# Passing the last two token groups through layer 1 together, 512 tokens wide, with 20 blocks of layer 2 converted beside it

## The chip, the core and the metric

The kernel runs on one core of one Trainium2 chip. The metric is device time in microseconds (us): the median of several executions. The core has five engines with a queue each: TensorE (PE, whose weight loads are shown as PEld), VectorE (DVE), ScalarE (ACT), GpSimd (POOL) and the sync engine (SP), which here only issues DMAs. Each queue runs in order. DMAs move data between DRAM and the on-chip memory; matmuls write to PSUM, of which there are eight banks of 512 fp32 columns.

## What is computed

Attention with a hash mask, and behind it two feed-forward layers, all in float32:

```python
# q, k, v: (2, 8, 768, 64); proj: (64, 6)
q_bucket, k_bucket = bits(q @ proj > 0), bits(k @ proj > 0)
scores = where(q_bucket == k_bucket, q @ k.T / 8, -1e9)
x = (softmax(scores) @ v).reshape(1536, 512)           # 1536 tokens
# layer 1: w_gate, w_val (512, 1536), w_out (1536, 512)
g = x @ w_gate
x = (g * sigmoid(g) * (x @ w_val)) @ w_out
# layer 2: w_in (512, 2048), w_out (2048, 512)
h = x @ w_in
out = (max(h, 0) + alpha * min(h, 0)) @ w_out
```

## The kernel before

**Attention.** There are 24 items: batch b, token group g of 256 tokens (three of them per batch) and pair p of heads, the pair running fastest. An item has two units, one per head, 48 in all. A unit goes through `banks` (three score banks in PSUM, each copied by ACT into the unit's tile `se`, in L280), `top` (maximum over keys on DVE, transposed on TensorE), `back` (subtract on DVE, exponential on ACT) and `values` (three pieces of the product with V, into the tile `po`). That makes eight steps per unit, and the parts of neighbouring units are interleaved. `prep` gives a pair its keys and hash rows. A pair's K comes three times: as one tile `nat` (SP's queue, L161) and twice into `kt` (POOL's queue); `rest_k` (L173) subtracts one from the other. For the pairs 1 to 3 of batch 0 `nat` is taken from the ring `se` of four buffers, in which the units' scores lie as well; for batch 1 it has a buffer of its own.

**Layer 1.** Six groups g of 256 tokens. Weights come as blocks of 128 x 512, 36 of them for layer 1 (24 for gate and value, 12 for output) and 32 for layer 2. Every product is made of three fp32r matmuls (`mm3`: high x high, high x low, low x high), so that a block has a high and a low half (tile `wb`, 512 KB, five buffers). In group 0 the blocks are converted from 64-bit storage: loaded as `raw` (ring `raw64` of two buffers), put together by `round64` (ACT L501, DVE L502 and L504, POOL L506), split (ACT L530; POOL or DVE L537) and stored to `scratch` in DRAM; the later groups load `wb` from there on SP's queue (L496). A step f of `stage1` uses two gate and value blocks and, from f = 3 on, one output block: 12 matmuls each, 432 in a group.

**What runs beside what.** Groups 0 to 4 are interleaved with attention: `stage1` yields 36 times in a group, and at each yield as many steps of attention are emitted as `RATES` says (2.0). A group begins when its tokens' attention is done. Besides, 18 blocks of layer 2 are converted early, six in each of the groups 2 to 4 (`EARLY`, `w_early`): `raw` load, `round64` into a tile `wt`, write to `whole` in DRAM (L525). Group 5 runs alone.

**Layer 2.** `stage2` passes three times over 512 tokens. Its 32 blocks are kept in `fin.w` (tile `w`): 18 are loaded from `whole` (L492), and the other 14 are loaded raw and converted in the first pass. In each pass a block is split again into `wb`.

**Order.** The Tile scheduler puts each engine's instructions into an order, by its own estimate. Instructions under `pin` keep the program's order; `ws.pin` is False while attention and layer 1 are interleaved, except for the early blocks. `w_ahead` issues weight loads three blocks ahead of use for blocks already in scratch.

## Time and profile before

| | us |
|---|---|
| median of 3 runs | 944.65 (941.87 to 944.72) |
| the profiled execution, its own time | 942.76 |
| its span, first to last instruction | 940.8 |
| TensorE busy (matmul) | 859.9 |
| VectorE busy | 593.6 |
| ACT busy | 442.6 |
| POOL busy | 389.3 |

A busy TensorE is not TensorE at its peak, since the matmuls are pipelined and their ends modelled: what a matmul costs is the distance from one start to the next. The stages in the profiled execution, by the first and the last matmuls of each: attention alone until 90.5 us, group 0 of layer 1 until 248.7, group 1 until 341.8, group 2 until 437.9, group 3 until 531.9, group 4 until 615.5, group 5 until 670.2, and the three passes of layer 2 until 762.7, 849.8 and 937. Attention's last matmul is in group 4. The table by stages below gives for each stretch its length, how long each engine was busy in it and with how many instructions, TensorE's granted clock and what the DMAs moved.

### The profile page before, as it was taken

The numbers are of one execution on the slowest core, as the hardware profiler recorded it, in microseconds if no ns is written. First come the engines' busy times: TensorE is split into PE (matmuls) and PEld (weight loads), VectorE is DVE, ScalarE is ACT, GpSimd is POOL, SyncE is SP. The second block draws the span as 40 slices with busy tenths as digits, with TensorE's granted clock in tenths as the row PEclk, the third lists the DMA queues.
The fourth block names the chain that finished last, engine by engine and source line by source line (L and its number), as shares of the span: only waits on it lengthen the run. The fifth ranks groups of instructions, "written<-read, shape, count | busy, mean of one in ns | idle before, by whom it ended". The sixth has DMA issues, their size and how long they took to land.

```text
span 940.8 us, 14038 instructions
## 1 busy us (share of the span) xinstructions
PE 859.9 (91%) x5248; PEld 765.6 (81%) x5248; DVE 593.6 (63%) x880; ACT 442.6 (47%) x784; POOL 389.3 (41%) x339
## 2 busy tenths in 40 slices
PE   4788787787999999999999997799999999999998
PEld 3577675676898999999999997789887788888886
DVE  4589999998665767677767752131489754335342
ACT  4588565745544554555555441121344433334331
POOL 4224666556433213233223312211478845444442
PEclk8799989989999999999999999899999999999999
DMA  9324767778999767878787867799934010001001
GB/s 236 73 68 134 227 232 218 251 232 268 321 305 298 228 214 242 279 262 280 246 269 235 269 224 290 278 358 362 366 114 155 1 46 1 0 1 45 1 1 45
DMA packets 70403, 180.53 MB, mean 192 GB/s; under 512 B 18880, under 2 KB 25024, under 8 KB 70336
## 3 DMA queue, kind: packets, MB, share of 16 engines
q1 hardware_dynamic: 68176, 174.10, 55.4%
q0 software_dynamic: 2016, 5.51, 2.9%
q8 instruction: 41, 0.67, 0.3%
q14 instruction: 26, 0.21, 0.1%
q10 hardware_dynamic: 144, 0.05, 0.0%
HBM read 152.88 MB, written 26.74 MB: 191 GB/s over the span
## 4 chain that ended last, share of the span: by engine, by line
PE 62%; DVE 16%; DMA 9%; POOL 5%; issue 4%; ACT 4%; SPq 1%; POOLq 0%; DVEq 0%; ACTq 0%
PE po L317 9%; PE gp L592 5%; PE gp L594 5%; PE gp L593 5%; PE hp L594 4%; PE op L599 4%; PE op L597 4%; PE op L598 4%; PE hp L592 4%; PE hp L593 4%; DMA nat<-in_k_dram 3%; DMA raw<-in_wblk_dram 3%; PE yp L594 3%; PE yp L592 2%; PE yp L593 2%
## 5 line engine op out<-in xcount | busy, mean ns | idle before, releaser
L587 POOL TENSOR_TENSOR gl<-ex,gh 128x256 fp32r<-128x256 f32 (+1 forms) x120 | 121.6, 1013 | 265.2 <-ACT gh L584 198.5
L592 PE MATMUL gp<-xh,wb 128*128 128x256 f32 x576 | 177.5, 308 | 18.4 <-ACT wb L530 11.4
L594 PE MATMUL gp<-xh,wb 128*128 128x256 f32 x576 | 168.3, 292 | 6.8 <-POOL wb L537 4.8
L593 PE MATMUL gp<-xl,wb 128*128 128x256 f32 x576 | 166.5, 289 | 1.8 <-POOL xl L346 1.8
L317 PE MATMUL po<-se,vv 128*128 128x256 f32 x576 | 149.8, 396 | 6.5 <-issue 3.5
L592 PEld LDWEIGHTS gp<-xh,wb 128*128 128x128 f32 x576 | 113.1, 196 | 24.7 <-ACT wb L530 14.5
L317 PEld LDWEIGHTS po<-se,vv 128*128 128x128 f32 x576 | 106.6, 199 | 19.8 <-ACT se L310 4.8
L594 PEld LDWEIGHTS gp<-xh,wb 128*128 128x128 f32 x576 | 113.3, 197 | 10.8 <-POOL wb L537 7.0
L593 PEld LDWEIGHTS gp<-xl,wb 128*128 128x128 f32 x576 | 113.5, 197 | 3.0 <-POOL xl L346 2.0
L584 ACT ACTIVATE gh<-ex 128x256 fp32r<-128x256 f32 (+1 forms) x120 | 60.2, 502 | 118.1 <-DVE ex L581 62.5
L310 ACT ACTIVATE se<-se 128x1536 f32<-128x1536 f32 x48 | 71.3, 1484 | 63.5 <-DVE se L305 63.3
L530 ACT ACTIVATE wb<-w 128x512 fp32r<-128x512 f32 x96 | 59.5, 628 | 83.4 <-PE hp L594 55.2
L592 PE MATMUL yp<-gh,wb 128*128 128x256 f32 x288 | 87.3, 305 | 11.6 <-DMA wb<-w 8.1
L537 POOL TENSOR_TENSOR wb<-w,wb 128x512 fp32r<-128x512 f32 x48 | 65.9, 1374 | 74.3 <-ACT wb L530 72.2
L506 POOL TENSOR_TENSOR wt<-wt,wr 128x512 int32<-128x512 int32 x54 | 76.5, 1416 | 48.5 <-DVE wt L504 31.1
L280 ACT ACTIVATE se<-S 128x512 f32<-128x512 f32 x144 | 80.1, 592 | 20.7 <-PE S L279 12.6
L572 DVE SCALAR_TENSOR_TENSOR ex<-ex,gp 128x256 f32<-128x256 f32 x72 | 30.1, 418 | 93.2 <-ACT ex L569 92.7
L537 DVE TENSOR_TENSOR wb<-w,wb 128x512 fp32r<-128x512 f32 x48 | 45.1, 940 | 66.5 <-ACT wb L530 66.5
L305 DVE SCALAR_TENSOR_TENSOR se<-se,mb 128x1536 f32<-128x1536 f32 x48 | 83.8, 1745 | 4.4 <-PE mb L300 4.2
L594 PE MATMUL yp<-gh,wb 128*128 128x256 f32 x288 | 82.2, 291 | 2.7 <-POOL wb L537 1.6
L593 PE MATMUL yp<-gl,wb 128*128 128x256 f32 x288 | 82.0, 286 | 0.5 <-POOL gl L587 0.5
L278 PE MATMUL S<-QA,kt 128*128 128x256 f32 x288 | 78.8, 301 | 1.9 <-ACT se L280 0.9
(92 smaller groups left out, 1943.5 us busy)
## 6 DMA issues: line engine op xcount, KB each, us to landing
wb<-w SPq DMA_DIRECT2D x180, 512.0 KB, 4.9
raw<-in_wblk_dram SPq DMA_DIRECT2D x68, 512.0 KB, 4.4
w<-wb SPq DMA_DIRECT2D x36, 512.0 KB, 5.2
qr<-in_q_dram SPq DMA_DIRECT2D x24, 256.0 KB, 4.4
kt<-in_k_dram POOLq DMA_DIRECT2D x14, 384.0 KB, 8.5
whole<-wt SPq DMA_DIRECT2D x18, 256.0 KB, 2.2
w<-whole SPq DMA_DIRECT2D x18, 256.0 KB, 5.4
nat<-in_k_dram SPq DMA_DIRECT2D x8, 384.0 KB, 7.9
```

Of the source, the lines that this page charges most:

```text
L278: nc.tensor.matmul(pt[:, i, :], lhsT=ka[:, sl], rhs=qa, start=True, stop=False)
L280: nc.scalar.activation(out=u.se[:, 2 * j:2 * j + 2, :], in_=pt, func=AF.Copy)
L305: nc.vector.scalar_tensor_tensor(out=u.se, in0=u.se, scalar=FLOOR, in1=u.mx[:, None, :].to_broadcast([P, NC, GQ]), op0=ALU.max, op1=ALU.su ...
L310: nc.scalar.activation(out=u.se, in_=u.se, func=AF.Exp, scale=SCALE)
L317: nc.tensor.matmul(it.po[:, u.x, :], lhsT=VV[it.b, it.p][:, kb, u.x * D:u.x * D + P], rhs=u.se[:, kb, :], start=kb == 0, stop=kb == NC - 1)
L506: pin(nc.gpsimd.tensor_tensor(out=a, in0=a, in1=r, op=ALU.add))
L537: eng.tensor_tensor(out=ready[i][:, 1, :], in0=wt.pop(i), in1=f32(ready[i])[:, 0, :], op=ALU.subtract)
L584: nc.scalar.activation(out=h, in_=ex, func=AF.Copy)
L587: nc.gpsimd.tensor_tensor(out=l, in0=ex, in1=f32(h), op=ALU.subtract)
L592: nc.tensor.matmul(pt, lhsT=h, rhs=ah, start=first, stop=False)
L593: nc.tensor.matmul(pt, lhsT=h, rhs=al_, start=False, stop=False)
L594: nc.tensor.matmul(pt, lhsT=l, rhs=ah, start=False, stop=last)
```

## The change

- `nat` of the pairs 1 to 3 of batch 0 is a buffer of the ring `raw64` (two buffers in the pool `wp`), no longer of `se`.
- `RATES` has four entries, 2.0, 2.4, 2.6 and 2.6; `EARLY` is 0, 0, 6, 6: four groups are interleaved with attention, and 12 blocks are converted early, in the groups 2 and 3.
- The groups 4 and 5 go through layer 1 together, in the new `stage1w`, after attention. Each matmul is 512 columns wide, 432 in all, with the weights loaded once for both groups.
- The other 20 blocks of layer 2 (`late`) are converted beside it by `w_late`, two per step f for ten steps, straight into `fin.w`, with two blocks' loads in the air; `w_load` does nothing for them. Loads and conversions there are pinned. The first pass of layer 2 converts nothing.

```diff
@@ -38,9 +38,9 @@
 
 PRIME = (32, 6)
 
-RATES = (2.0, 2.0, 2.0, 2.0, 2.0)
-
-EARLY = (0, 0, 6, 6, 6, 0)
+RATES = (2.0, 2.4, 2.6, 2.6)
+
+EARLY = (0, 0, 6, 6)
 
 
 @with_exitstack
@@ -156,8 +156,10 @@
 
     def load_k(it):
 
-        tag, n = ("se", at.nse) if it.b == 0 else ("nat", 1)
-        it.nat = at.sm.tile([P, S], F32, tag=tag, name="nat", bufs=n)
+        if it.b == 0:
+            it.nat = wp.tile([P, S], F32, tag="raw64", name="nat", bufs=RAWB)
+        else:
+            it.nat = at.sm.tile([P, S], F32, tag="nat", name="nat", bufs=1)
         nc.sync.dma_start(out=it.nat, in_=kview2(it))
         nc.gpsimd.dma_start(out=KA(it)[0:D], in_=kview(it))
         nc.gpsimd.dma_start(out=KB(it)[0:D], in_=kview(it))
@@ -463,7 +465,8 @@
 
     o2 = order2()
     early = o2[:sum(EARLY)]
-    seq = order1() * (B * NG) + o2 * NP2
+    late = [w for w in o2 if w not in early]
+    seq = order1() * (len(RATES) + 1) + o2 * NP2
     NWT = len(seq)
     fresh = [w not in seq[:i] for i, w in enumerate(seq)]
     new = [n or w >= F2I for n, w in zip(fresh, seq)]
@@ -488,8 +491,10 @@
 
     def w_load(i):
         w = seq[i]
-        if fresh[i] and w in early:
-            nc.sync.dma_start(out=fin.w[:, w - F2I, :], in_=whole[w - F2I])
+        if w in late:
+            pass
+        elif fresh[i] and w in early:
+            pin(nc.sync.dma_start(out=fin.w[:, w - F2I, :], in_=whole[w - F2I]))
         elif fresh[i]:
             raw[i] = raw_load(w)
         elif w < F2I:
@@ -513,6 +518,17 @@
             wt[i] = wp.tile([P, 512], F32, tag="wt", name="wt", bufs=WB[0])
         if i in raw:
             round64(raw.pop(i), wt[i].bitcast(I32))
+
+    def w_late():
+
+        rs = []
+        for w in late + [None] * RAWB:
+            if len(rs) == RAWB or w is None:
+                r, v = rs.pop(0)
+                round64(r, fin.w[:, v - F2I, :].bitcast(I32))
+            if w is not None:
+                rs.append((raw_load(w), w))
+            yield
 
     def w_early():
 
@@ -659,6 +675,43 @@
             nc.scalar.activation(out=xh[:, 2 * i:2 * i + 2, :], in_=yp[i], func=AF.Copy)
             nc.vector.tensor_tensor(out=xl[:, 2 * i:2 * i + 2, :], in0=yp[i], in1=f32(xh)[:, 2 * i:2 * i + 2, :],
                                     op=ALU.subtract)
+
+    def stage1w(t0):
+
+        xh, xl = [t[:, :, t0:t0 + W] for t in X]
+        gs = {}
+        conv = w_late()
+        for f in range(F1 + D1):
+            for _ in range(-(-(len(late) + RAWB) // F1)):
+                next(conv, 0)
+            if f < F1:
+                ps = []
+                for i in range(2):
+                    tag = ("G", "M", "G", "po")[(2 * f + i) % 4]
+                    pt = at.ps.tile([P, W], F32, tag=tag, name="gp2", bufs=at.nb[tag])
+                    w = w_next()
+                    for kk in range(KD):
+                        mm3(pt, (w[0][:, kk, :], w[1][:, kk, :]), xh[:, kk, :], xl[:, kk, :], kk == 0, kk == KD - 1)
+                    ps.append(pt)
+                ex = tmp()
+                gs[f] = [fin.pool.tile([P, W], F32R, tag=t, name=t, bufs=D2 + 1) for t in ("gh2", "gl2")]
+                gate_tanh(ps[0], ex)
+                gate_mul(ps[0], ex)
+                gate_val(ps[1], ex)
+                split_h(gs[f][0], ex)
+                split_l(gs[f][0], gs[f][1], ex)
+            if f >= D1:
+                fo = f - D1
+                h, l = flat(w_next())
+                a, b_ = gs.pop(fo)
+                if fo == 0:
+                    yp = [at.ps.tile([P, W], F32, tag=t, name="yp2", bufs=at.nb[t]) for t in "SSYY"]
+                for e in range(KD):
+                    sl = slice(e * P, (e + 1) * P)
+                    mm3(yp[e], (h[:, sl], l[:, sl]), a, b_, fo == 0, fo == F1 - 1)
+        for e in range(KD):
+            nc.scalar.activation(out=xh[:, e, :], in_=yp[e], func=AF.Copy)
+            nc.vector.tensor_tensor(out=xl[:, e, :], in0=yp[e], in1=f32(xh)[:, e, :], op=ALU.subtract)
 
     def stage2(t0):
 
@@ -764,8 +817,8 @@
         pass
     fin.pool = ctx.enter_context(tc.tile_pool(name="fin", bufs=1))
     fin.w = fin.pool.tile([P, 2 * F2, 512], F32, name="w2")
-    for _ in stage1(B * NG - 1):
-        pass
+    ws.pin = True
+    stage1w(len(RATES) * GQ)
     for n in range(NP2):
         stage2(n * W)
```

What the scheduler makes of it, at two places.

The start, on SP: the loads behind the first two items. nat_154, nat_200 and nat_208 are the K tiles of the pairs 1 to 3, nat_2248 that of batch 1, vv the tiles of V, qr those of Q, al alpha. Before:

```order
L155 DMA vv_160<-in_v_dram 128x6x64 x2
L161 DMA nat_200<-in_k_dram 128x768
L161 DMA nat_208<-in_k_dram 128x768
L167 DMA qr_216<-in_q_dram 128x2x256
L122 DMA al_69<-in_alpha_dram 128x16
L161 DMA nat_2248<-in_k_dram 128x768
L155 DMA vv_204<-in_v_dram 128x6x64 x2
L155 DMA vv_212<-in_v_dram 128x6x64 x2
L155 DMA vv_218<-in_v_dram 128x6x64 x2
L167 DMA qr_299<-in_q_dram 128x2x256
```

After:

```order
L155 DMA vv_160<-in_v_dram 128x6x64 x2
L163 DMA nat_200<-in_k_dram 128x768
L122 DMA al_69<-in_alpha_dram 128x16
L169 DMA qr_216<-in_q_dram 128x2x256
L163 DMA nat_2248<-in_k_dram 128x768
L155 DMA vv_204<-in_v_dram 128x6x64 x2
L155 DMA vv_212<-in_v_dram 128x6x64 x2
L155 DMA vv_218<-in_v_dram 128x6x64 x2
L163 DMA nat_208<-in_k_dram 128x768
L169 DMA qr_299<-in_q_dram 128x2x256
```

nat_208 moved from the place behind nat_200 to one behind the six loads of V.

The start, on ACT: the score copies of the first unit (se_222) and of the second (se_256), and the exponentials (L310 before, L312 after). Before:

```order
L280 ACTIVATE se_222<-S_230 128x512
L280 ACTIVATE se_222<-S_237 128x512
L178 ACTIVATE QA_340<-qr_216 128x512
L310 ACTIVATE se_222<-se_222 128x1536
L280 ACTIVATE se_256<-S_257 128x512
L280 ACTIVATE se_256<-S_263 128x512
L280 ACTIVATE se_256<-S_274 128x512
L201 ACTIVATE kt1_128<-mk_280 12x384 x2
```

After:

```order
L282 ACTIVATE se_222<-S_230 128x512
L282 ACTIVATE se_222<-S_237 128x512
L282 ACTIVATE se_256<-S_257 128x512
L282 ACTIVATE se_256<-S_263 128x512
L282 ACTIVATE se_256<-S_274 128x512
L180 ACTIVATE QA_340<-qr_216 128x512
L312 ACTIVATE se_222<-se_222 128x1536
L312 ACTIVATE se_256<-se_256 128x1536
```

The second unit's copies moved ahead of the first unit's exponential.

The end of the last group that runs beside attention and the start of what follows it, on SP. w18 to w35 and then w0, w1, ... are layer 1's blocks in scratch, raw64 the raw loads, whole the write of an early block. Before, from group 4 to group 5:

```order
L525 DMA whole_109<-wt_6415 128x512
L496 DMA wb_6458<-w33_106 128x1024
L496 DMA wb_6473<-w34_107 128x1024
L486 DMA raw64_6495<-in_wblk_dram 128x1024
L496 DMA wb_6497<-w35_108 128x1024
L496 DMA wb_6511<-w0_73 128x1024
L496 DMA wb_6531<-w1_74 128x1024
L496 DMA wb_6545<-w2_75 128x1024
L525 DMA whole_109<-wt_6525 128x512
L496 DMA wb_6568<-w3_76 128x1024
L496 DMA wb_6583<-w4_77 128x1024
```

After, from group 3 to the wide stage:

```order
L501 DMA wb_5873<-w2_75 128x1024
L541 DMA whole_109<-wt_5853 128x512
L489 DMA raw64_5896<-in_wblk_dram 128x1024
L489 DMA raw64_5898<-in_wblk_dram 128x1024
L501 DMA wb_5901<-w3_76 128x1024
L501 DMA wb_5916<-w4_77 128x1024
L489 DMA raw64_5943<-in_wblk_dram 128x1024
L489 DMA raw64_5950<-in_wblk_dram 128x1024
L501 DMA wb_5953<-w5_78 128x1024
L501 DMA wb_5968<-w6_79 128x1024
L489 DMA raw64_5995<-in_wblk_dram 128x1024
L489 DMA raw64_6002<-in_wblk_dram 128x1024
```

Where weight loads alone stood after the last early block, two raw loads now stand ahead of each step's weight loads, and the last writes to whole come in group 3.

## Rows read from the trace of the kernel before

**Rows 1.** Busy by stretch: length, PE, PEld, DVE, ACT, POOL (instructions), clock, DMA share, GB/s.

```profile
20.00:43.00 23.00, 15.53 (x56) 10.23 (x55) 11.81 (x15) 8.94 (x14) 6.16 (x3) 0.67 0.51 130
43.00:90.50 47.50, 41.46 (x245) 35.17 (x244) 43.44 (x69) 39.89 (x70) 13.62 (x12) 0.96 0.27 87
90.50:248.70 158.20, 126.45 (x753) 108.49 (x753) 145.96 (x202) 95.09 (x169) 98.41 (x81) 0.91 0.77 243
...
341.80:437.90 96.10, 94.92 (x706) 91.33 (x705) 71.46 (x113) 53.97 (x101) 30.90 (x28) 1.00 0.75 255
437.90:531.90 94.00, 93.97 (x702) 90.92 (x701) 67.55 (x108) 51.02 (x91) 27.77 (x25) 1.00 0.76 255
561.00:615.50 54.50, 42.68 (x312) 41.61 (x311) 12.97 (x29) 11.37 (x26) 13.52 (x15) 0.91 0.75 281
615.50:670.20 54.70, 52.63 (x434) 51.98 (x433) 11.50 (x26) 10.93 (x28) 8.90 (x13) 1.00 0.97 356
622.00:662.00 40.00, 39.95 (x333) 39.78 (x332) 8.43 (x20) 7.59 (x19) 6.30 (x9) 1.00 0.98 359
670.20:762.70 92.50, 88.64 (x386) 71.76 (x386) 72.65 (x81) 40.06 (x69) 68.62 (x48) 1.00 0.34 118
762.70:849.80 87.10, 87.10 (x386) 72.13 (x385) 36.24 (x50) 31.52 (x51) 41.16 (x32) 1.00 0.04 13
```

**Rows 2.** DMA issues, 622 to 662 us: count, size, median us to landing.

```profile
wb<-w SPq DMA_DIRECT2D x27, 512.0 KB, 5.2
```

**Rows 3.** The chain that ended last, in order of time: start, us, what.

```profile
556.01 5.23 PE po L317 x24
```

**Rows 4.** Timeline of SP's queue, 545 to 690 us: start, us, what is issued.

```profile
566.36 0.32 SPq L525 DMA_DIRECT2D whole<-wt  x1
...
567.26 2.60 SPq L496 DMA_DIRECT2D wb<-w  x4
...
615.59 0.32 SPq L525 DMA_DIRECT2D whole<-wt  x1
```

**Rows 5.** Instructions by line, PE, 561 to 616: busy, mean ns, idle before.

```profile
L592 PE MATMUL gp<-xh,wb 128*128 128x256 f32 x61 | 19.1, 313 | 4.5 <-DMA wb<-w 4.5
...
L592 PE MATMUL yp<-gh,wb 128*128 128x256 f32 x44 | 13.2, 299 | 7.3 <-DMA wb<-w 7.3
```

**Rows 6.** Timeline of PE, 570 to 576 us, after a wait for a weight block.

```profile
573.92 0.35 PE L592 MATMUL yp<-gh,wb 128*128 128x256 f32 x1 [2.98 <-DMA wb<-w]
...
575.06 0.42 PE L593 MATMUL yp<-gl,wb 128*128 128x256 f32 x1
575.27 0.41 PE L594 MATMUL yp<-gh,wb 128*128 128x256 f32 x1
```

**Rows 7.** Timeline of the start, 15 to 40 us: start, us, engine, line, what.

```profile
15.62 11.03 SPq L155 DMA_DIRECT2D vv<-in_v_dram  x6
...
18.19 1.24 ACT L280 ACTIVATE se<-S 128x512 f32<-128x512 f32 x2 [0.43 <-PE S L279]
...
26.25 5.46 PE L317 MATMUL po<-se,vv 128*128 128x256 f32 x12 [3.47 <-issue]
...
31.81 1.58 ACT L280 ACTIVATE se<-S 128x512 f32<-128x512 f32 x3 [5.66 <-PE po L317]
...
32.92 0.69 DVE L284 TENSOR_TENSOR m<-se 128x512 f32<-128x512 f32 x1 [5.42 <-ACT se L280]
...
37.63 1.74 DVE L305 SCALAR_TENSOR_TENSOR se<-se,mb 128x1536 f32<-128x1536 f32 x1
```

**Rows 8.** Instructions by line, 670 to 763 us: layer 2's first pass, with conversions.

```profile
L506 POOL TENSOR_TENSOR w<-w,wr 128x512 int32<-128x512 int32 x14 | 20.2, 1440 | 10.0 <-DVE w L504 5.7 <-ACT wr L501 2.3 <-ACT wb L530 2.0
L504 DVE SCALAR_TENSOR_TENSOR w<-raw,w 128x512 int32<-128x512 int32 x14 | 17.4, 1244 | 0.3
L502 DVE TENSOR_SCALAR w<-raw 128x512 int32<-128x512 int32 x14 | 11.4, 813 | 2.6 <-DMA raw<-in_wblk_dram 2.5
L581 DVE SCALAR_TENSOR_TENSOR ex<-hp,ex 128x512 f32<-128x512 f32 x16 | 11.0, 688 | 0.4
```

## The prediction

> **What bounds the kernel now.** I read the span by stages first [rows 1], then who ends the waits in the stages that lose time [rows 3 to 6], then the start [rows 7]. The reader is to see that TensorE is the bound from 248.7 us on, except in three stretches.
>
> Two prices come first. From 622 to 662 us one group passes layer 1 alone: 333 matmuls of 256 columns in 40.00 us, 0.120 us each. The second pass of layer 2 needs 87.10 us for 384 matmuls of 512 columns (16 blocks x 4 x 3, twice), 0.2268 us each [rows 1].
>
> Group 3 of layer 1, with attention beside it (437.9 to 531.9 us), is TensorE and nothing else: busy 93.97 of 94.00 us [rows 1]. Its own 432 matmuls are 51.8 us, and 42.2 us belong to 72 steps of attention. VectorE is busy 67.55 us there. Group 0 (90.5 to 248.7) is bound by VectorE, 145.96 of 158.2 us, and so is the tail of the start: 43.44 of 47.5 us from 43 to 90.5 [rows 1].
>
> Attention ends at 561.2 us (the last run of matmuls into po, [rows 3]). From there to 615.5 us only 312 matmuls run, 37.4 us of work in 54.5; from 615.5 to 670.2 us 434, 52.1 us in 54.7 [rows 1]. The 17.1 us lost in the first stretch have one shape. A converted block is written to DRAM (whole<-wt) by SP's queue, five of them there, from 566.36 to 615.59 us; the queue stands at that write until GpSimd has finished the block, and the weight loads (wb<-w) stand behind it [rows 4]. TensorE then waits for wb, 7.3 + 4.5 us in all [rows 5], and after such a wait of 2.98 us its matmuls start 0.21 us apart (575.06, 575.27) [rows 6], the lower of the clock's two levels; the granted clock is 0.91 over the stretch [rows 1]. So one such block costs 17.1 / 5 = 3.4 us. The first pass of layer 2 takes 92.50 us, 5.4 over the second [rows 1]: TensorE waits there for weights whose split stands behind conversions on VectorE and GpSimd.
>
> **The change part by part.** All sums stand against the profiled execution, 942.76 us (span 940.8 and 2.0 around it). The median of the runs is 944.65, 1.9 above it, and one of the three is 0.9 below, so the sum may sit some 2 us low.
>
> *K of three pairs in the raw64 ring.* Before, the three early K tiles and the first unit's scores fill the four buffers of se, so the second unit's scores are copied only at 31.81 us, when ACT has idled 5.66 us for the first unit's po, and VectorE idled 5.42 us for that [rows 7]. In the new order these copies follow directly on the first unit's, which end at 19.4 us: 12 us sooner. Still in its place is the first unit's po, from 26.25 to 31.7 us on TensorE [rows 7] at a granted clock of 0.67 over 20 to 43 us [rows 1], and the next pair's hash behind it. What goes is VectorE's work on the second unit, five instructions from 32.92 to 39.37 us [rows 7], 0.69 + 0.69 + 0.42 + 0.42 + 1.74 = 4.0 us, that now falls into idle time, and about 1 us of waits in its chain. From 20 to 43 us VectorE worked 11.81 of 23 us, after that 91% [rows 1], so whatever its start gains lasts. Between 0 and the idle 11.2 us I take 5, which is nearest to the 4.0 just counted. The cost: the load of the last early K (nat_208) now waits for a buffer and stands behind six loads of V whose issue takes 11.03 us, from 15.62 to 26.65 us [rows 7]. Issued at 26.7 and with some 5 us to land [rows 2] it is there at about 32 us, an estimate; the instructions behind it on VectorE are the next pair's hash, which need that pair's matmuls, not before 31.8 us. If it lands later, the 5 us shrink.
>
> *Attention 2.4 to 2.6 steps per step of layer 1.* In the program's order 1851 of the 2592 matmuls of layer 1 stand before the last one of attention; in the changed order 1575 of the 256-wide kind. TensorE is the bound, so attention ends 276 x 0.120 = 33.1 us earlier, and nothing is saved by that itself. VectorE gets denser: even if all of group 2's 71.46 us [rows 1] scaled by 1.3, it would be 92.9 us beside 51.8 + 1.3 x 42.2 = 106.7 us of TensorE, 87%. That is under the 92% of group 0, where TensorE did idle. I charge 1 us, bounded by 0 and by 3.5 (group 2's 96.10 - 94.92 = 1.2 us idle [rows 1], in each of some 96 of 280 us).
>
> *What is left after attention.* Before: 741 matmuls, 88.9 us of work, in 109.2 us: 20.3 us lost. After: 153 matmuls of 256 columns (18.4 us) and 432 of 512 columns (98.0 us), 116.4 us of work, where the same was 33.1 + 88.9 = 122.0: 5.7 us saved by the width (864 x 0.120 = 103.7 against 98.0). The trace shows a fixed part of 2 x 0.120 - 0.2268 = 0.013 us per matmul that wider ones pay half as often [rows 1].
>
> The Trainium skill, "TensorE: Matmul & The Clock Gate", section Back-to-back issue gap, gives N/2.4 + 2.5 ns for a matmul at full clock. By that an estimate of the saving is 432 x 2.5 ns = 1.1 us, and the sum would come 4.6 us higher, at 921. The trace does not agree with its fixed part (13 ns against 2.5), and the measured one is used.
>
> Lost time after: three whole<-wt writes still stand behind attention's end in SP's order, but the last has only 512-wide blocks ahead of it (12 x 0.2268 = 2.7 us each, three loaded), which cover it. Two at 3.4 us are 6.8 us; bounds 3.4 and 10.3 (one and three).
>
> *Twenty blocks converted beside the wide stage.* One step of it is 36 matmuls, 8.2 us; the first three lack the output block, 5.4 us. Per step two blocks: VectorE 2 x 0.69 us for the gates (the nearest form of that width) and 2 x (0.81 + 1.24) for the conversions, 5.5 us; GpSimd three additions of 1.44, 4.3 us [rows 8]. Both lie under 8.2 us of TensorE and are just even with it in the first three steps. SP: each raw load waits until VectorE and ACT have read the block two before it, which comes behind the last step's gate, and the next step's weight load stands behind both. From the end of a value matmul: gate 0.7, conversions to +2.8 and +4.8, weights landing 5.2 us later [rows 2], +10; needed at +10.9, four blocks of 2.7 us later (in the first three steps three blocks, +8.2). So a wait of a us or so in some of the first steps, none later. DMA: five blocks of 524288 bytes per step, 2.62 MB in 8.2 us = 321 GB/s, under the 359 moved from 622 to 662 us [rows 1]. I charge 2 us. The lower bound is 0; the upper is the 281 GB/s of 561 to 615.5 us [rows 1], 9.3 us per step, +1.2 in each of ten steps: 12 us. If the cover of 8.2 us were gone, the ten pairs would cost VectorE's 10 x 4.1 = 41 us.
>
> *First pass of layer 2.* Its 14 conversions are gone, and so 5.4 us of waits [rows 1]; loads from whole fall from 18 to 12. I take 5.0 (0.4 left for a late first load), bounds 3 and 5.4.
>
> Sum: 942.8 - 5 (start) + 1 (denser attention) - 5.7 (width) - (20.3 - 6.8 - 2 = 11.5) (waits after attention) - 5.0 (first pass) = 916.6, say **917 us**.
>
> **The rivals.** *Late blocks stall like early ones* (slower than before). If SP's queue stands at each raw load as it stands at whole<-wt, twenty blocks cost 3.4 us each: 914.6 + 68 = 983 us. It decides from (942.8 - 914.6) / 20 = 1.4 us a block. For it: the loads do wait on VectorE. Against: there is no write that waits for GpSimd; a raw load waits for reads that end some 5 us after the gate, where the writes stood (615.59 - 566.36) / 4 = 12.3 us apart [rows 4], the time of a block from its load to its end. 5 in 100.
>
> *DMA is the bound of the wide stage*, at the 281 GB/s above: 916.6 - 2 + 12, about 927 us. For it: bursts of five loads per step, writes are gone though. 17 in 100.
>
> *The change at the start does not do what it says*: the late K holds VectorE's queue as long as the second unit gained, or longer by up to 3 us: 922 to 925. 10 in 100.
>
> *More than forecast*: the start gives 9 us and only one early block stalls (3.4): 909. 13 in 100.
>
> **How the numbers follow.** My forecast, 917, has 55 in 100. The range 905 to 932 us takes in the rivals at 909, 925 and 927 with some 5 us for bounds that fall together; it leaves out the first rival and sums where several terms go to their ends. About 0.3% (2.8 us) can be told from no change here. Of the first rival's 5, 4 are slower by more and 1 falls within; one more within comes from the DMA case with all else at its bad end. So faster 0.94, same 0.02, slower 0.04.
>
> **What would show it.** Right: second unit's score copies near 19.5 us and group 0 starting near 85; attention ending near 523; group 3's tail losing 5 to 8 us; the wide stage 98 to 101 us long with the clock at 1.0 and DMA near 320 GB/s; three passes of 87 us. Wrong: TensorE idling for wb in every wide step, a granted clock under 1 there, VectorE waiting for nat in the start, or matmuls of groups 1 to 3 waiting for VectorE.

## The result, and the profile after

The changed kernel takes 918.43 us (median, 916.04 to 920.38) beside 944.68 for the kernel before, a ratio of 0.9727 [0.9696, 0.9757]. Measured once more on another occasion it was 915.93 us, ratio 0.9708 [0.9693, 0.9722]. So it is 2.7 to 2.9% faster, 26 to 27 us. The prediction was 917 us in a range of 905 to 932. The time came out as forecast; two of its terms, the tail of group 3 and the wide stage, did not, in opposite directions.

The profiled execution of after took 920.38 us (span 918.6), the highest of its runs. Busy time by stretch, as in [rows 1] (length, then PE, PEld, DVE, ACT, POOL with instructions, granted clock, DMA share, GB/s); the stretches are two parts of the start, groups 0, 1 and 2, group 3 with and without attention, the wide stage and two passes of layer 2:

```profile
20.00:43.00 23.00, 16.66 (x78) 12.12 (x77) 15.20 (x20) 11.04 (x19) 4.97 (x3) 1.00 0.55 139
43.00:89.10 46.10, 40.62 (x226) 33.91 (x226) 40.70 (x64) 36.58 (x64) 13.50 (x11) 0.93 0.27 89
89.10:248.70 159.60, 122.90 (x747) 106.19 (x747) 140.41 (x200) 95.56 (x169) 98.90 (x81) 0.94 0.75 238
248.70:350.40 101.70, 100.04 (x732) 94.46 (x731) 64.05 (x108) 56.96 (x106) 28.77 (x29) 1.00 0.82 261
350.40:457.50 107.10, 107.10 (x787) 103.27 (x786) 77.79 (x131) 63.93 (x113) 31.34 (x30) 1.00 0.70 234
457.50:526.60 69.10, 68.26 (x484) 64.71 (x483) 49.07 (x83) 36.26 (x63) 15.25 (x16) 1.00 0.66 228
526.60:547.70 21.10, 18.84 (x153) 18.32 (x152) 7.03 (x15) 6.02 (x14) 6.96 (x8) 1.00 0.86 310
547.70:653.30 105.60, 99.35 (x435) 80.69 (x434) 58.72 (x70) 30.99 (x53) 46.48 (x34) 1.00 0.83 302
653.30:740.40 87.10, 87.10 (x386) 72.16 (x385) 37.23 (x52) 31.93 (x52) 41.18 (x32) 1.00 0.01 2
740.40:827.40 87.00, 87.00 (x386) 72.06 (x385) 36.22 (x50) 31.41 (x51) 41.19 (x32) 1.00 0.03 13
```

Read three things. Group 2, with 2.6 steps of attention per step, is TensorE from end to end, 107.10 of 107.10 us, as group 3 was before. The first pass of layer 2 is as short as the second, 87.1 us where it was 92.5. And the clock is 1.00 from group 1 on. What is still lost stands in two rows: 21.1 us for the 18.4 us of work left of group 3, and 105.6 us for the 98.0 of the wide stage.

Against the two profiles, by the program's marks (first layer-1 matmul of group 1, last matmul into po, end of layer 1, end of the first pass):

| from, to | before | after | difference | forecast |
|---|---|---|---|---|
| start to group 1 | 248.8 | 248.7 | -0.1 | -5 |
| to attention's end | 312.1 | 277.7 | -34.4 | -33.1 + 1 |
| to layer 1's end | 109.3 | 127.0 | +17.7 | +33.1 - 5.7 - 11.5 |
| first pass | 92.4 | 87.1 | -5.3 | -5.0 |
| the other two passes, to the end of the span | 178.2 | 178.1 | -0.1 | 0 |

The third row splits into the tail of group 3, 21.3 us where 18.4 + 6.8 = 25.2 were forecast, and the wide stage, 105.6 where 98 + 2 = 100 were. The experiments ask why the wide stage loses 105.6 - 98.0 = 7.6 us, whether the start is really worth nothing, and which parts of the change carry the gain.

In the wide stage TensorE waits for weights and once for a conversion (engine, line, what it waited for, us in total, times, longest):

```profile
PE gp L608 <- DMA wb<-w: 5.7, 4, 2.3
PE gp L608 <- DVE w L507: 0.6, 1, 0.6
```

SP's queue over the same steps shows what stands ahead of these weights (start, us until the last of the group is issued, what):

```profile
561.06 3.30 SPq L489 DMA_DIRECT2D raw<-in_wblk_dram  x2
564.45 0.86 SPq L501 DMA_DIRECT2D wb<-w  x2
568.29 3.34 SPq L489 DMA_DIRECT2D raw<-in_wblk_dram  x2
571.73 1.33 SPq L501 DMA_DIRECT2D wb<-w  x3
574.24 3.63 SPq L489 DMA_DIRECT2D raw<-in_wblk_dram  x2
577.96 2.68 SPq L501 DMA_DIRECT2D wb<-w  x3
```

Two raw loads take 3.3 to 3.6 us, since the second stands until the second block of the step is converted. VectorE and GpSimd beside the middle pair:

```profile
566.35 0.69 DVE L591 SCALAR_TENSOR_TENSOR ex<-ex,gp 128x512 f32<-128x512 f32 x1 [1.79 <-PE gp L610]
566.96 0.42 DVE L507 TENSOR_SCALAR w<-raw 128x512 int32<-128x512 int32 x1
567.41 0.69 DVE L509 SCALAR_TENSOR_TENSOR w<-raw,w 128x512 int32<-128x512 int32 x1
568.02 1.52 DVE L507 TENSOR_SCALAR w<-raw 128x512 int32<-128x512 int32 x1
569.58 1.66 DVE L509 SCALAR_TENSOR_TENSOR w<-raw,w 128x512 int32<-128x512 int32 x1
...
567.79 1.48 POOL L603 TENSOR_TENSOR gl<-ex,gh 128x512 fp32r<-128x512 f32 x1 [2.39 <-ACT gh L600]
569.22 1.47 POOL L511 TENSOR_TENSOR w<-w,wr 128x512 int32<-128x512 int32 x1
```

The same two instructions take 0.42 and 0.69 us for the first block and 1.52 and 1.66 for the second, which run beside GpSimd's split of the gate (L603) and its addition for the first block (L511). The weights issued behind that pair, from 571.73 us, are what TensorE waits for at 577.32 us. Its four waits for weights:

```profile
563.31 0.47 PE L608 MATMUL gp<-xh,wb 128*128 128x512 f32 x1 [1.68 <-DMA wb<-w]
569.29 0.47 PE L608 MATMUL gp<-xh,wb 128*128 128x512 f32 x1 [0.26 <-DMA wb<-w]
577.32 0.47 PE L608 MATMUL gp<-xh,wb 128*128 128x512 f32 x1 [2.35 <-DMA wb<-w]
595.28 0.47 PE L608 MATMUL gp<-xh,wb 128*128 128x512 f32 x1 [1.39 <-DMA wb<-w]
```

### The profile page after: what moved, and what is told of

Read it like the earlier page. It is cut to its first block, busy times and chain, and to the rows that moved or that the text cites. A ratio compares the mean times of both kernels' runs of the same rounds, so it can differ in the third digit from the quotient of the medians.

```text
span 918.6 us, 13016 instructions
## 1 busy us (share of the span) xinstructions
PE 845.2 (92%) x4816; PEld 737.4 (80%) x4816; DVE 570.9 (62%) x856; ACT 441.6 (48%) x760; POOL 377.0 (41%) x327
## 4 chain that ended last, share of the span: by engine, by line
PE 69%; DVE 12%; ACT 5%; DMA 5%; POOL 5%; issue 3%; SPq 0%; POOLq 0%; DVEq 0%; ACTq 0%
PE po L319 9%; PE gp L608 6%; PE gp L609 6%; PE gp L610 6%; PE op L614 5%; PE hp L609 5%; PE op L613 5%; PE hp L608 5%; PE op L615 5%; PE hp L610 5%; DMA wb<-w 3%; POOL wt L511 3%; PE yp L610 3%; PE yp L608 3%; PE yp L609 3%
## 5 line engine op out<-in xcount | busy, mean ns | idle before, releaser
L603 POOL TENSOR_TENSOR gl<-ex,gh 128x512 fp32r<-128x512 f32 (+1 forms) x108 | 116.6, 1079 | 220.9 <-ACT gh L600 162.7
L608 PE MATMUL gp<-xh,wb 128*128 128x256 f32 (+1 forms) x480 | 155.9, 325 | 22.2 <-ACT wb L546 12.1
L610 PE MATMUL gp<-xh,wb 128*128 128x256 f32 (+1 forms) x480 | 150.6, 314 | 7.4 <-DVE wb L553 3.8
L609 PE MATMUL gp<-xl,wb 128*128 128x256 f32 (+1 forms) x480 | 148.7, 310 | 1.7 <-POOL xl L348 1.7
L608 PEld LDWEIGHTS gp<-xh,wb 128*128 128x128 f32 x480 | 93.1, 194 | 33.4 <-ACT wb L546 15.1
L600 ACT ACTIVATE gh<-ex 128x512 fp32r<-128x512 f32 (+1 forms) x108 | 57.8, 535 | 109.0 <-DVE ex L597 46.7
L610 PEld LDWEIGHTS gp<-xh,wb 128*128 128x128 f32 x480 | 93.6, 195 | 14.1 <-DVE wb L553 5.1
L312 ACT ACTIVATE se<-se 128x1536 f32<-128x1536 f32 x48 | 71.3, 1485 | 61.6 <-DVE se L307 61.4
L609 PEld LDWEIGHTS gp<-xl,wb 128*128 128x128 f32 x480 | 93.7, 195 | 6.0 <-POOL xl L348 1.9
L511 POOL TENSOR_TENSOR wt<-wt,wr 128x512 int32<-128x512 int32 x48 | 67.7, 1410 | 54.7 <-DVE wt L509 29.8
L307 DVE SCALAR_TENSOR_TENSOR se<-se,mb 128x1536 f32<-128x1536 f32 x48 | 83.8, 1745 | 5.0 <-PE mb L302 4.7
L608 PE MATMUL yp<-gh,wb 128*128 128x256 f32 (+1 forms) x240 | 76.0, 318 | 7.6 <-ACT wb L546 5.7
L281 PE MATMUL S<-qb,kt 76*128 76x256 f32 x288 | 75.8, 295 | 2.4 <-ACT kt L203 2.2
L610 PE MATMUL yp<-gh,wb 128*128 128x256 f32 (+1 forms) x240 | 72.6, 308 | 4.9 <-POOL wb L553 3.4
L608 PE MATMUL hp<-xh,wb 128*128 128x512 f32 x192 | 74.7, 389 | 0.0
```

Of the source, the lines that this page charges most:

```text
L281: nc.tensor.matmul(pt[:, i, :], lhsT=kb[:, sl], rhs=qb, start=False, stop=True)
L307: nc.vector.scalar_tensor_tensor(out=u.se, in0=u.se, scalar=FLOOR, in1=u.mx[:, None, :].to_broadcast([P, NC, GQ]), op0=ALU.max, op1=ALU.su ...
L312: nc.scalar.activation(out=u.se, in_=u.se, func=AF.Exp, scale=SCALE)
L511: pin(nc.gpsimd.tensor_tensor(out=a, in0=a, in1=r, op=ALU.add))
L603: nc.gpsimd.tensor_tensor(out=l, in0=ex, in1=f32(h), op=ALU.subtract)
L608: nc.tensor.matmul(pt, lhsT=h, rhs=ah, start=first, stop=False)
```

## The experiments

Ratios are to the kernel before, each to runs of it on the same chip.

### Raw loads behind the weight loads

```diff
-                round64(r, fin.w[:, v - F2I, :].bitcast(I32))
+                round64(r[0], fin.w[:, v - F2I, :].bitcast(I32))
             if w is not None:
-                rs.append((raw_load(w), w))
+                r = []
+                behind.append(lambda r=r, w=w: r.append(raw_load(w)))
+                rs.append((r, w))
...
+            while behind:
+                behind.pop(0)()
```

The last two lines stand at the end of each wide step.

> The kernel after, but each wide step issues its two raw loads on SP behind the step's weight loads instead of ahead of them; conversions stand where they stood. Theory (SP's queue): the wide stage loses 7.5 us because weight loads stand behind the second raw load, which waits 3.3 to 3.6 us for VectorE; with the weights one step ahead of that wait the stage falls from 105.5 us to 98.0 of work plus about 2, and the kernel from 918.4 to about 913. Rival (bandwidth: the same bytes must still pass at 302 GB/s or so): stage 105 us, kernel 918. Second rival (raw blocks now come too late and the first pass waits for the last conversions): stage 100, first pass over 88, kernel 915 to 918.

Measured: 909.29 us, ratio 0.9653 [0.9631, 0.9675], 5 to 7 us under after. The busy times of its wide stage (columns as above):

```profile
546.90:646.30 99.40, 98.25 (x434) 80.89 (x433) 46.15 (x70) 31.62 (x53) 46.00 (x34) 1.00 0.88 320
```

The waits in that stage:

```profile
PE gp L612 <- DMA wb<-w: 1.1, 1, 1.1
```

The stage takes 99.4 us. One wait for a weight block is left. Same bytes, same conversions, another order on one queue: the order alone gave back 6.2 of the 7.6 us, one profile against the other. The bandwidth rival falls: the stage now moves 320 GB/s instead of 302. So does the rival of the late conversions, since the first pass takes 87.0 us here too.

### Raw loads from GpSimd's queue

```diff
-    def raw_load(w):
+    def raw_load(w, eng=nc.sync):
...
-        pin(nc.sync.dma_start(out=t, ...
+        pin(eng.dma_start(out=t, ...
...
-                rs.append((raw_load(w), w))
+                rs.append((raw_load(w, nc.gpsimd), w))
```

> The kernel after, but the twenty raw loads of the wide stage are issued from GpSimd's queue, each behind the addition that follows the conversion whose buffer it takes, so that SP's queue holds weight loads alone there. Theory (SP's queue): no weight load waits for VectorE any more; wide stage 98 to 100 us, kernel about 913 or a little less than with the raw loads behind. Rival (bandwidth): 918, with waits for wb in the same places. Second rival (issuing costs GpSimd time that its split of the gate needs): new waits of TensorE for the gate's low part, 915 to 920.

Measured: 908.73 us, ratio 0.9644 [0.9621, 0.9666], 6 to 8 us under after. TensorE has no idle time left in the wide stage:

```profile
541.90:639.90 98.00, 98.00 (x435) 81.18 (x434) 46.59 (x70) 31.84 (x53) 53.51 (x53) 1.00 0.92 324
```

On GpSimd a raw load stands behind an addition that could only start when the raw block had been read, so that its buffer is free when its turn comes; its issue takes 0.7 us of an engine that is busy for 53.5 of 98 us. GpSimd's timeline:

```profile
565.90 1.28 POOL L511 TENSOR_TENSOR w<-w,wr 128x512 int32<-128x512 int32 x1 [1.15 <-DVE w L509]
567.13 0.71 POOL L489 DMA_DIRECT2D raw<-in_wblk_dram  x1
568.61 1.28 POOL L511 TENSOR_TENSOR w<-w,wr 128x512 int32<-128x512 int32 x1 [0.77 <-ACT ex L585]
```

The theory holds: with the raw loads off SP's queue all of the 7.6 us of the wide stage are gone. The rival of GpSimd's time falls, since no wait for the gate's low part appears.

### Late conversions without GpSimd's addition

```diff
-    def round64(t, a):
+    def round64(t, a, add=True):
...
-        pin(nc.gpsimd.tensor_tensor(out=a, in0=a, in1=r, op=ALU.add))
+        if add:
+            pin(nc.gpsimd.tensor_tensor(out=a, in0=a, in1=r, op=ALU.add))
...
-                round64(r, fin.w[:, v - F2I, :].bitcast(I32))
+                round64(r, fin.w[:, v - F2I, :].bitcast(I32), add=False)
```

> The kernel after without GpSimd's addition in the twenty late conversions (the low bits are left out of those blocks). Theory (VectorE is slowed by GpSimd's addition of the block before): the second block's two VectorE instructions fall from 1.5 and 1.7 us to 0.4 and 0.7 as for the first block, the two raw loads of a step stand about 1 us apart on SP instead of 3.3 to 3.6, waits for wb mostly go, stage about 100 us, kernel about 913 to 915. Rival (bandwidth): VectorE's times fall too, but the stage stays at 105 us and the kernel at 918. Rival (the distance is the landing of the second raw block, not VectorE): the loads stay 3.3 us apart, 918.

Measured: 914.34 us, ratio 0.9699 [0.9678, 0.9721], not told apart from after with certainty (0.9708 and 0.9727). The wide stage takes 102.2 us in its trace, where after took 105.6 in one profile and 103 in another. Half of the mechanism is seen. VectorE's two conversion instructions from 555 to 640 us, grouped by line (busy us, mean ns of one, idle before), in after:

```profile
L509 DVE SCALAR_TENSOR_TENSOR w<-raw,w 128x512 int32<-128x512 int32 x20 | 22.5, 1127 | 0.7
L507 DVE TENSOR_SCALAR w<-raw 128x512 int32<-128x512 int32 x19 | 17.2, 905 | 2.9 <-DMA raw<-in_wblk_dram 2.9
```

And without the addition:

```profile
L507 DVE TENSOR_SCALAR w<-raw 128x512 int32<-128x512 int32 x18 | 15.8, 880 | 1.4 <-DMA raw<-in_wblk_dram 1.3
L509 DVE SCALAR_TENSOR_TENSOR w<-raw,w 128x512 int32<-128x512 int32 x18 | 12.5, 693 | 0.6
```

L509 falls to its undisturbed 693 ns, so the addition was what slowed it. L507 stays at 880, against my expectation of 0.4 us: it runs beside GpSimd's split of the gate, which is still there. Both engines' timelines of this kernel:

```profile
580.12 1.53 DVE L507 TENSOR_SCALAR w<-raw 128x512 int32<-128x512 int32 x1
...
579.95 1.42 POOL L604 TENSOR_TENSOR gl<-ex,gh 128x512 fp32r<-128x512 f32 x1 [8.09 <-ACT gh L601]
```

So issuing two raw loads takes 2.4 us instead of 3.3, where about 1 was expected, and the gain is small.

### The wide stage undone, and undone with the raw loads on GpSimd

```diff
-    seq = order1() * (len(RATES) + 1) + o2 * NP2
+    seq = order1() * (B * NG) + o2 * NP2
...
-    stage1w(len(RATES) * GQ)
+    conv = w_late()
+    for g in range(len(RATES), B * NG):
+        for k, _ in enumerate(stage1(g)):
+            if k % 3 == 0:
+                next(conv, 0)
```

> The kernel after with the wide stage undone: the last two groups pass layer 1 one after the other, 256 tokens wide, each weight block loaded twice, and the twenty late conversions are spread beside them, one per half step. My prediction counted the width as 5.7 us of TensorE time alone (864 x 0.120 against 432 x 0.2268): by that the two groups take 104 us of work plus the same losses, kernel about 924. Rival (the width pays by halving the weight traffic): 72 weight blocks and 20 raw ones of 524288 bytes are 48.2 MB; at the 302 to 359 GB/s seen they take 134 to 160 us in place of 105.5, kernel 947 to 973.

Measured: 970.28 us, ratio 1.0297 [1.0266, 1.0328], slower than the kernel before. The two groups take 156.1 us (104 us of work) at 313 GB/s, with the clock at 0.92:

```profile
546.70:702.80 156.10, 119.32 (x867) 114.88 (x865) 48.40 (x92) 33.20 (x74) 45.90 (x44) 0.92 0.84 313
```

TensorE waits for weights there, 35 us in all:

```profile
PE gp L608 <- DMA wb<-w: 21.5, 11, 3.5
PE yp L608 <- DMA wb<-w: 13.6, 6, 3.6
```

That is what the rival of bytes said, but the queue's order could say it as well. The second kernel parts them: it is this one with raw_load on nc.gpsimd.

> The kernel narrow with the late raw loads issued from GpSimd's queue, as in raw_pool. Theory (two narrow groups with twenty conversions are bound by DMA bytes): 48.2 MB at 310 to 330 GB/s stay at 146 to 156 us, kernel 955 to 970. Rival (narrow lost its time to the order on SP's queue): the two groups fall to 104 to 115 us, kernel 918 to 930.

Measured: 940.15 us, ratio 0.9974 [0.9944, 1.0003]. Neither number that I had written down: the two groups take 124.3 us.

```profile
547.40:671.70 124.30, 111.96 (x867) 105.69 (x867) 45.98 (x92) 33.59 (x75) 54.91 (x65) 1.00 1.01 394
```

What TensorE still waits for there:

```profile
PE gp L608 <- DMA wb<-w: 7.4, 13, 1.9
PE yp L608 <- DMA wb<-w: 3.7, 9, 0.8
```

So 156.1 - 124.3 = 32 us of what narrow lost came with the raw loads on SP's queue. That this was order there, as in the wide stage, and not also the use of one queue instead of two, is the likely reading; no narrow kernel with only the order changed was run. Behind that bytes seem to be the bound, with the DMA engines busy all the time (1.01) at 394 GB/s, more than the 359 I had taken for what they reach. Between narrow_pool and raw_pool lie 31 us, which is what the width is worth with the queue out of the way. The stages account for 124.3 - 98.0 = 26.3 of it: 5.7 are TensorE's fixed part, and I put the other 20 down to the second reading of the weights: 22 of TensorE's waits there, 11.1 us by this view, are for weight blocks. The remaining 5 us stand ahead of group 1 (249.2 and 244.1 us), in the same program, a spread that is told of below.

### The twenty blocks in the first pass of layer 2

```diff
-    late = [w for w in o2 if w not in early]
+    late = []
...
-                next(conv, 0)
+                if late:
+                    next(conv, 0)
```

> The kernel after with the twenty late blocks converted in the first pass of layer 2 instead of beside the wide stage. Theory (the wide stage loses its 7.5 us to the conversions' raw loads, and the first pass of before lost 5.4 us to 14 conversions): wide stage 98 to 99 us, first pass 87 + 5.4 x 20 / 14 = 94.7 us, kernel 918.4 - 6.8 + 7.7 = about 919. Rival (the first pass has room for 14 conversions but not for 20: its losses grow faster than their number): first pass over 97 us, kernel 922 or more. Rival (the wide stage loses to its own weight loads, not to the conversions): wide stage still over 103.

Measured: 934.89 us, ratio 0.9914 [0.9888, 0.9940], a miss for my 919; the rival that the pass has no room for 20 conversions had it, with 922 or more. The wide stage takes 97.8 us as forecast, so its own weight loads cost it nothing; the first pass takes 110.9 us. Both stretches:

```profile
547.60:645.40 97.80, 97.80 (x434) 80.98 (x433) 20.32 (x30) 19.51 (x33) 17.98 (x14) 1.00 0.65 224
645.40:756.30 110.90, 94.68 (x386) 70.28 (x385) 67.36 (x91) 42.63 (x72) 70.76 (x52) 1.00 0.27 89
```

TensorE's longest waits in the first pass:

```profile
PE hp L608 <- ACT wb L546: 7.9, 7, 1.3
PE op L614 <- POOL wb L553: 5.5, 8, 0.7
```

Twenty conversions cost 23.9 us there, 1.2 us each, where 14 cost 5.4 in the kernel before [rows 1], 0.4 each. The price does not grow in proportion to their number. TensorE waits for halves of the weight split, but the split in its turn waits for the conversion, whose last instruction is GpSimd's addition (L511). ScalarE's half of the split for every other block, as it recurs in the middle of the pass:

```profile
694.46 0.63 ACT L546 ACTIVATE wb<-w 128x512 fp32r<-128x512 f32 x1 [2.79 <-POOL w L511]
702.75 0.63 ACT L546 ACTIVATE wb<-w 128x512 fp32r<-128x512 f32 x1 [2.78 <-POOL w L511]
```

Two blocks take 8.29 us there, where TensorE needs 24 x 0.2268 = 5.44 for them. No engine but TensorE is busy for more than 64% of the pass (GpSimd 70.76 of 110.90 us), so it is not one engine's work that sets this pace. The chain that ended last runs there in a circle, from VectorE's conversion and its share of the activation through ScalarE and GpSimd's addition to the split and back to VectorE. What would shorten it was not tested. Beside the wide stage the same twenty cost 7.6 us, or nothing with the loads on GpSimd.

### Attention at 2.0 throughout

```diff
-RATES = (2.0, 2.4, 2.6, 2.6)
+RATES = (2.0, 2.0, 2.0, 2.0)
```

> The kernel after with attention at 2.0 steps per step of layer 1 in all four groups, so that what is left of attention after group 3 runs alone ahead of the wide stage. My reading (density saves nothing by itself, it only lets attention end inside group 3): about 12.6 us of TensorE work of attention stand alone, at VectorE's pace of 0.8 us a step for some 21 steps, 17 to 25 us, so 5 to 12 us longer: 923 to 930. Rival (denser attention itself cost time in groups 1 to 3, as my 1 to 3.5 us assumed, and more): 918 or less.

Measured: 922.07 us, ratio 0.9774 [0.9743, 0.9806], 4 to 6 us over after and just under the 923 to 930 that I had written. What is left of attention runs alone for 22.2 us, from 526.8 to 549 us, where 17 to 25 were reckoned:

```profile
526.80:549.00 22.20, 19.89 (x100) 16.45 (x99) 13.17 (x21) 10.53 (x15) 1.48 (x2) 1.00 0.27 99
```

That is 9.6 us more than the 12.6 us of TensorE work that I had reckoned for it. The 2.7 us that after loses in the tail of group 3 are saved here, since attention lasts to the end of that group, so some 7 us are left for 4 to 6 measured. The density saves this stretch's idle time, and nothing else is seen of it.

### K staging undone, and alone

In the first kernel load_k of after goes back to the se ring; the second is the kernel before with load_k of after.

> The kernel after with K of the first three pairs back in the se ring; all else as changed. My prediction gave the K staging 5 us: by that the kernel is 5 us slower than after, a ratio of 0.978 to before. Rival (what the trace of after shows: group 0 starts 1.4 us sooner than before and group 1 no sooner): the same time as after within 1.5 us, ratio 0.971 to 0.974.

Measured: 918.10 us, ratio 0.9752 [0.9728, 0.9776], between the 0.978 and the 0.971 to 0.974 that I had written down.

> The kernel before with K of the first three pairs staged in the raw64 ring, and nothing else changed. My prediction: 5 us faster than before, ratio 0.9947. Rival (the gain is lost again before group 1): within 0.2% of before.

Measured: 938.22 us, ratio 0.9960 [0.9938, 0.9982], 3.8 us under before (1.7 to 5.8).

> The changed kernel itself once more, beside the next three on one chip. Both theories of the K staging: 0.970 to 0.975 of before. If the staging is worth 2 to 4 us, as the timed runs with K undone (ratio 0.9752) and K alone (0.9960) say together, the ratio here is near 0.972; if it is worth nothing, near 0.975. In its trace group 1 may start anywhere between 244 and 249 us, since kernels with the same program up to there have shown that spread.

Measured: 0.9708 [0.9693, 0.9722]. Undone against this, the staging is worth 0.0044 of 943, 4.1 us, with the two intervals together about 1.5 to 6.8. Against the first measurement of after (0.9727) it is 2.4 us, with an interval from -1.3 to 6.0 that does not exclude nothing. Alone, its interval begins at 1.7 us. Together they speak for some 4 us, and the rival that it is worth nothing, which I had read out of the profile of after, falls: one profiled execution could not show it. Eleven profiles of kernels whose program is the same up to group 1 start that group anywhere from 244.1 to 249.2 us. In the three that start it soonest, up to 244.7 us (raw_pool, pool_both and rates2), the granted clock from 43 to 87 us is 1.00; in seven of the others, after among them, it is 0.92 to 0.96 there, and raw_behind has 1.00 and starts it at 247.5. A difference of 4 us in that part needs timed runs.

The steps of the start are seen in the trace of after nonetheless, beside [rows 7]:

```profile
20.18 0.60 ACT L282 ACTIVATE se<-S 128x512 f32<-128x512 f32 x1 [0.26 <-PE S L281]
...
26.34 4.71 PE L319 MATMUL po<-se,vv 128*128 128x256 f32 x12
30.89 0.38 PE L302 MATMUL mb<-ident,mq 128*128 128x128 f32 x2
...
31.31 1.75 DVE L307 SCALAR_TENSOR_TENSOR se<-se,mb 128x1536 f32<-128x1536 f32 x1 [3.31 <-PE mb L302]
```

The second unit's scores are copied by 20.8 us (by 33.4 before, 31.81 + 1.58), but its subtraction on VectorE (L307) waits for mb, which stands behind the first unit's po on TensorE: of the 4.0 us that I had counted as moved into idle time, 1.75 stay behind po.

### What else stands on SP: writes, and the last early K

Two steps onward from raw_pool. The first puts the twelve writes of early blocks on GpSimd's queue, behind the addition they wait for; the second also loads K of the fourth pair (nat_208) into the first pair's tile, so that its load stands ahead of the loads of V.

```diff
-            nc.sync.dma_start(out=whole[w - F2I], in_=t)
+            nc.gpsimd.dma_start(out=whole[w - F2I], in_=t)
```
```diff
-        if it.b == 0:
+        if it.b == 0 and it.p < 3:
```

> The kernel raw_pool with the twelve writes of early blocks (whole<-wt) issued from GpSimd's queue as well, each right behind the addition it waits for, so that SP's queue stands at nothing but weight buffers. Theory (each write that SP stands at delays the weight loads behind it): the tail of group 3, where 21.3 us were taken for 18.4 of work, falls to 18.5 to 19, and the kernel from 908.7 to about 906. Rival (the tail loses to the DMA traffic of its weight loads, 312 GB/s there): the tail stays at 21, kernel 908.7. Second rival (GpSimd's issue delays its splits or the conversions of groups 2 and 3): those groups longer by a us or two, 909 to 911.

Measured: 907.87 us, ratio 0.9633 [0.9608, 0.9658], not told apart from raw_pool's 0.9644. In the trace the tail of group 3 takes 20.1 us, with 21.3 in raw_pool; DMA moves 324 GB/s there. From the last matmul into po to the first one of what follows it is 20.4 us here and in the next kernel, and 21.3 to 22.0 in the nine profiles with the writes on SP, so the difference is clear of their spread. The theory gets one of the 2.7 us; the rest of the tail is not the writes' doing.

```profile
521.50:541.60 20.10, 18.95 (x154) 18.47 (x152) 7.48 (x15) 6.24 (x14) 7.80 (x9) 1.00 0.87 324
```

> The kernel pool_both with the last early K (nat_208) loaded into the first pair's own K tile, so that its load stands ahead of the six loads of V on SP instead of behind them (26.9 us in after) and no longer waits in the raw64 ring. Theory (what the staging could give was held back by that load, as my prediction feared): its copy on VectorE moves ahead of the second unit's subtraction, group 0 starts 2 to 4 us sooner, kernel 904 to 906. Rival (the start is held by the first unit's po on TensorE at the low clock and by the next pair's hash): group 0 at 87 to 89 us as before, kernel 907 to 909.

Measured: 907.05 us, ratio 0.9612 [0.9593, 0.9630], the fastest of all, but not told apart from pool_both. Its group 0 starts at 89.1 us, no sooner, so the theory of the late K finds no support. Its group 1 starts at 242.1 us, sooner than in any of the eleven profiles above; whether 2 us are gained inside group 0, as this one profile and the two ratios suggest, stays open.

## Why the prediction was right, step by step

**K staging, -5.** Timed at some -4 (1.5 to 6.8 undone, 1.7 to 5.8 alone; less against the first measurement of after). The mechanism was right in that the second unit's copies moved 12.6 us forward (done at 20.8 instead of 33.4 us); the size was near. Of the 4.0 us behind it, though, 1.75 stayed behind the first unit's po, so that 2.2 of the 4.0 are seen to move, and where the rest of the timed gain comes from was not traced. The fear for the late K was not borne out by moving it.

**Denser attention, +1.** Attention's end came 34.4 us sooner from group 1's start, where 33.1 - 1 was forecast: the charge was not needed. VectorE at 77.79 of 107.10 us in group 2, 73%, is far from binding, less than the 87% that I had bounded it by. rates2 confirms the other half: the rate saves nothing in the groups, it only keeps a remainder from running alone.

**Width, -5.7.** It holds: 432 matmuls in 98.0 us in raw_pool, 0.2268 us each, where 864 narrow ones are 103.7. As a statement on the width it was incomplete, as narrow_pool shows: with conversions beside it, halving the weight traffic is worth some 20 us more. The sum did not miss it, since it counted the conversions beside the wide stage only. The formula that the prediction set beside the measured part, from the Trainium skill, "TensorE: Matmul & The Clock Gate", section Back-to-back issue gap, is given there for a single matmul by itself, not for a stream of them, so its 921 was no forecast for this stage.

**Tail of group 3, 6.8.** Mis-sized: 2.7 us. TensorE waited for weights three times, 2.3 us in all, and the granted clock stayed at 1.00. The 3.4 us per write came from a stretch with 11.8 us of waits and a granted clock of 0.91 together [rows 1, 5, 6]; 41 of its matmuls start 0.20 to 0.23 us apart instead of 0.12, 4 of the 17.1 us. Nor are all of the 2.7 us the writes': without them on SP's queue the tail still takes 20.1 us (pool_both), so they cost some 1.2 us here. Why the waits are so much shorter than before was not tested.

**Twenty blocks beside the wide stage, 2.** Mis-sized: 7.6 us in one profile, about 5 in two others (after_again and k_undone, 103 us for the stage). Place and mechanism were named: weights behind raw loads that wait for VectorE, in the first steps. In the third step, from the end of a value matmul at 566.3 the conversions end at 571.24 (+4.9, forecast +4.8), the weights are issued from 571.73 and are there at 577.32 (+11.0, forecast +10), and TensorE wants them at 574.8 (+8.5, forecast +8.2). My own two numbers gave a wait of 1.8 us in each of the first three steps, 5.4 together, and I summed them up as one wait or so. What failed is that last step, the addition: the raw loads of these three steps gave waits of 1.68, 0.26 and 2.35 us, 4.3 together. I also had no wait in later steps; one of 1.39 us came at 595.28. The landing of weights was longer too, 6.2 us in the median (5.2 in [rows 2]). The rival of bandwidth gave 12 us, and its reason was wrong: the traffic went from 302 to 320 GB/s as soon as the order on SP was changed.

The conversion's price on VectorE, 0.81 + 1.24 us a block, was a mean over two kinds, 0.42 + 0.69 alone and 1.5 + 1.7 beside GpSimd, and only the second stood on the path. The Trainium skill, "SBUF — State Buffer", section Who interferes with whom, says that an instruction of VectorE with two inputs from SBUF, or in a mode that uses both of its ports, shares a port pair with GpSimd and one of them waits, while one with a single SBUF input outside such modes does not. The traces agree: L509, with two inputs from SBUF, takes 1.66 us beside GpSimd and 0.69 alone, and the gate's instructions, with one input in PSUM, take 0.69 either way. L507 has one input and still takes 1.53 and 0.42, so by that rule it runs in a mode with both ports, which no trace here shows.

**First pass, -5.0.** Measured -5.3.

In the sum, for the profile of after: the start showed 4.9 less than forecast, density and tail 2.3 and 3.9 more, the wide stage 5.6 less, the pass 0.3 more. 916.6 + 4.9 - 2.3 - 3.9 + 5.6 - 0.3 = 920.6, beside 920.38. That the total was met is in part such cancelling, and so in part luck. By the timed runs the start misses by about 1 us and not by 4.9; the rest is probably the spread of such profiles.

## What to carry to other kernels

A queue that issues transfers in order is a resource like an engine: ask of every transfer put on it what it waits for and what stands behind it, and put a load that waits for a reader on the queue of an engine that is behind that reader anyway. A wider stage gains twice, by paying the fixed part of a matmul half as often and by reading the weights once instead of twice, and the second was worth more here, where other transfers shared the time. When a duration on the path is a mean, look whether it is two durations, and when a forecast wait recurs, add it up step by step.

## What the runs showed of the hardware

DMA reached 394 GB/s over 124 us with loads from SP's and GpSimd's queues together (share 1.01, narrow_pool). In the kernel before, with these loads on SP's queue alone, it was 359 over 40 us [rows 1], and 375 over the 20 us from 660 to 680.

Waits of 3.6 us at most, 35 us in all, went with a granted clock of 0.92 in narrow; waits of 2.35 us at most, 6.3 in all, left it at 1.00 in the wide stage of after. In narrow 156.1 - 104 of work - 35 of waits leaves 17 us. The lower clock is some 10 of them: 104 of its matmuls start 0.20 to 0.23 us after the one before instead of 0.12, 9.8 us together. The rest was not traced.

The same program up to group 1 took 244.1 to 249.2 us in eleven profiles, a spread of 5.1 us, as much as most of the terms of this prediction are worth.
